# A state-space scan with a GELU feed-forward: another order of the steps, and the chunk-decay product in the y bank

## The chip, the cores and the metric

The kernel runs on one core of one Trainium2 chip. The metric is device time in microseconds (us), from one launch to its end. The engines are named as in the profile: PE (TensorE, with PEld for its weight loads), DVE (VectorE), ACT (ScalarE), POOL (GpSimd), and SP, which here only issues DMAs.

## The reference

A Mamba-2 style scan in chunks, for 4 batches and 8 heads over 768 positions (head size 32, state size 16), and then a feed-forward layer with the tanh form of GELU on the 3072 tokens of 256 features (hidden size 2048). Cut to what matters:

```python
cum = np.cumsum(log(clip(a)), axis=-1)                 # within a chunk
M = einsum('bhin,bhjn->bhij', C, B) * exp(cum_i - cum_j) * causal
y = M @ x + (C @ state) * exp(cum_i)
state = exp(sum(la)) * state + sum_j B_j x_j * exp(cum_end - cum_j)
h = y_as_tokens @ w_in
out = (0.5 * h * (1 + tanh(sqrt(2/pi) * (h + 0.044715 * h**3)))) @ w_out
```

## The kernel before

The scan uses chunks of 128 positions: 6 chunks for each batch, 24 in all, numbered `gc`. Two chunks are a unit `u` (0 to 11), three units a batch. The decays are folded into B and C by scaling them with running products of `a`, so each chunk needs only plain products. For a unit:

- `G.u` (L595): products of B and C, eight of 256 columns, into the banks `ga` and `gb`
- `M.u.0`, `M.u.1` (L605): DVE masks `ga` and `gb` with the triangle, into `m`
- `D.u` (L628): the chunk's contribution to the state; `S.u.k` (L674, L676) adds it to the decayed state and `SP.gc` (L683) makes the masked copy that the next chunk uses
- `Y.u` (L650, L659): y of both chunks, into the bank `yb`; `yev.u` copies it to `xm` (L666)
- `s1.u.i`, i from 0 to 7 (L709): first layer, four products of 256 columns into a buffer of the ring `hp` (two PSUM buffers); `gelu.u.i` (L713) takes it to `gT`
- `s2.u.k.q` (L727): second layer for chunk k, four products into the single buffer `o_ps` (or into `yb` for some late chunks); `oev.gc` copies it out and `store.gc` writes it

Units 0 and 1 have their own start. `XX.u` (L563) and `XD.u` (L573) unpack x and form the first state contributions for chunks 0 to 3, with copies `xn.c`; they take buffers of `hp` and `o_ps`. `tw` and `ew` transpose the scaled B and C of chunks 0 to 3; `GE` and `ME` (L610, L616) bring half of unit 0's mask through ACT and POOL. Chunks 4 and 5 come by `tp2`, `recip1`, `mul1.0`, `mul1.1`, `T1`, `bh1`, `ce1`, `N1` and `bn1`. `R` (L331) is the running product over `a`; `pe` (L385, L387), `pp` (L393) and `pend` form the decay of each whole chunk, spread over partitions by a product.

Batch 1 scales B and C with `mul.1.i` (L475) and turns them on PE (`T.1.i`, `E.1.i`, `N.1`, `bn.1`). Batches 2 and 3 turn them by way of memory: `store_s` (L497) writes the scaled tile to scratch, `turn_s` (L504) and `load_s` (L509) read it back turned and plain, `F` (L515) splits C by even and odd heads. The weights come in eight loads of 512 KB (`load_wi.q`, L190, `load_wo.q`, L194), each into a buffer of its own, and are cast to bf16 in halves (`wi.q.k`, `wo.q.k`). `castx.u` casts x.

The order of all this is written out by hand in the string `ORDERED`: the steps are issued in the sequence in which they stand there, and an engine runs its own in that sequence. `:A`, `:D` or `:P` behind a name puts the step on ACT, DVE or POOL. `~n` issues filler products of n times 128 columns into `yb` (L697); `+n` does so ahead of an `s1`, in its own buffer. A buffer's next user waits for the readers of the last.

Of the kernel before, what the change touches and what calls it, by code (L numbers as in the profile page):

```python
# [45 lines left out]
gelu.4.6 yev.5.0.2:D SP.12 s2.4.0.0.o s2.4.0.1.o s1.4.7 D.7 Y.6 G.7 gelu.4.7 load_bc.3.0 load_bc.3.1
mul.3.0 mul.3.1 S.7.0 S.7.1 load_x.9 s1.5.0 gelu.5.0 s2.4.0.2.o s2.4.0.3.o oev.8:A M.7.1
castx.8.None:A M.7.0 s1.5.1 s1.5.2 gelu.5.1 store_s.3.1 yev.6.0.2:D SP.14 s2.4.1.0.o s2.4.1.1.o
s1.5.3 gelu.5.2 s2.4.1.2.o s1.5.4 s2.4.1.3.o gelu.5.3 gelu.5.4 oev.9:A s1.5.5 D.8 Y.7 gelu.5.5
store_s.3.0 load_x.10 load_x.11 store.5 G.8 S.8.0 s1.5.6 s1.5.7 castx.9.None:D gelu.5.6 M.8.1  # L50
gelu.5.7 store.6 s2.5.0.0.o s2.5.0.1.o turn_s.3.0 s1.6.0 s1.6.1 s2.5.0.2.o s2.5.0.3.o gelu.6.0
gelu.6.1 oev.10:D SP.16 s1.6.2 s1.6.3 gelu.6.3 gelu.6.2 s2.5.1.0.o s2.5.1.1.o s2.5.1.2.o s2.5.1.3.o
load_s.3 store.9 turn_s.3.1 s1.6.4 s1.6.5 M.8.0 yev.7.0.2:A oev.11:A SP.15 store.8 gelu.6.4
s2.6.0.0.o F.3 s2.6.0.1.o gelu.6.5 s1.6.6 s1.6.7 gelu.6.6 Y.8 D.9 G.9 S.9.0 SP.18 S.9.1 store.7
gelu.6.7 s2.6.0.2.o s2.6.0.3.o castx.11.None:D oev.12:D s1.7.0 s1.7.1 s2.6.1.0.o gelu.7.0 s2.6.1.1.o
gelu.7.1 s1.7.2 s1.7.3 s2.6.1.2.o s2.6.1.3.o SP.19 oev.13:D M.9.0 gelu.7.2 M.9.1 castx.10.None:P
gelu.7.3 s1.7.4 s1.7.5 s2.7.0.0.o s2.7.0.1.o gelu.7.4 s1.7.6 gelu.7.5 yev.8.0.2:A s2.7.0.2.o s1.7.7
gelu.7.6 Y.9 D.10 S.10.0 S.10.1 G.10 gelu.7.7 M.10.0 s2.7.0.3.o yev.9.0.2:A oev.14:A s1.8.0 s1.8.1
s2.7.1.0.o s2.7.1.1.o gelu.8.0 gelu.8.1 SP.20 s1.8.2 s1.8.3 M.10.1 gelu.8.2 s2.7.1.2.o s2.7.1.3.o
gelu.8.3 s1.8.4 s1.8.5 Y.10 oev.15:A gelu.8.4 D.11 S.11.0 G.11 gelu.8.5 s1.8.6 store.15 s1.8.7  # L60
gelu.8.6 s2.8.0.0.o s2.8.0.1.o gelu.8.7 store.11 store.10 s1.9.0 gelu.9.0 s1.9.1 s2.8.0.2.o
s2.8.0.3.o gelu.9.1 M.11.1 M.11.0 oev.16:D SP.21 SP.22 yev.10.0.2:A s1.9.2 s1.9.3 gelu.9.2
s2.8.1.0.o s2.8.1.1.o gelu.9.3 s1.9.4 store.14 s1.9.5 gelu.9.4 s2.8.1.2.o s2.8.1.3.o gelu.9.5 s1.9.6
# [899 lines left out]
```

## Time and profile before

| | us |
|---|---|
| median of 3 runs | 117.64 |
| runs | 116.85 to 118.97 |
| span of the profiled execution | 115.1 |
| PE busy in it | 109.4 |
| ACT, DVE, POOL busy | 75.1, 68.7, 15.1 |

The span runs from the first to the last instruction of one profiled execution; the time of that execution as the runs count theirs is not recorded, and the median of the timed runs stands 2.5 us above the span. A row of a timeline gives start, length (from the first to the end of the last of a group), engine, line, operation, tiles and shapes, the count, and in brackets how long the engine was idle and what ended it. Starts and lengths are in us.

### The profile page before, as it was taken

To read this page: it belongs to the slowest core of one execution; us is meant where nothing else is said; L and a number is where in the kernel's file an instruction comes from. 1 tells how busy PE (TensorE), PEld (TensorE's weight loads), DVE (VectorE), ACT (ScalarE), POOL (GpSimd) and SP (SyncE) were. 2 spreads that over 40 slices of the span, in tenths; PEclk is the share of its full clock that TensorE was granted. 3 is DMA by queue.
4 is the path that set the end of the run, shared out by engine and by line. 5 is a ranking of instruction groups with operands and counts; after the bars stand their busy time and mean duration, and the time that the engine had idled before them with its cause. 6 is when DMAs were issued, how large, how long until landed. Compare 5 with 4: busy or idle time off the path is not lost.

```text
span 115.1 us, 3372 instructions
## 1 busy us (share of the span) xinstructions
PE 109.4 (95%) x1425; PEld 92.2 (80%) x1425; DVE 68.7 (60%) x135; ACT 75.1 (65%) x149; POOL 15.1 (13%) x32
## 2 busy tenths in 40 slices
PE   6999799999999999999999999999999999999990
...
DMA packets 43006, 15.97 MB, mean 139 GB/s; under 512 B 36656, under 2 KB 41456, under 8 KB 42992
## 3 DMA queue, kind: packets, MB, share of 16 engines
...
q10 hardware_dynamic: 144, 0.08, 0.4%
...
## 4 chain that ended last, share of the span: by engine, by line
PE 82%; DMA 8%; SPq 4%; POOL 1%; issue 1%; ACT 0%
PE hp L709 36%; PE o_ps L727 33%; DMA wf<-in_moe_w_out_dram 8%; PE yb L727 3%; PE ga L595 3%; PE yb L650 2%; PE yb L659 2%; SPq L190 1%; PE hp L628 1%; SPq L162 1%; SPq L159 1%; SPq L150 1%; POOL w_out_sb L316 1%; POOL w_in_sb L316 1%; SPq L183 1%
## 5 line engine op out<-in xcount | busy, mean ns | idle before, releaser
L713 ACT ACTIVATE gT<-hp 128x512 bf16<-128x512 f32 x96 | 53.3, 595 | 24.5 <-PE hp L709 24.0
L709 PE MATMUL hp<-xm,w_in_sb 128*128 128x256 bf16 x384 | 51.9, 273 | 0.5 <-ACT pend L314 0.3
L727 PE MATMUL o_ps<-w_out_sb,gT 128*128 128x256 bf16 x352 | 46.4, 273 | 0.0
L709 PEld LDWEIGHTS <-w_in_sb 128*128 128x128 bf16 x384 | 41.2, 114 | 3.2 <-issue 1.7
L727 PEld LDWEIGHTS <-gT 128*128 128x128 bf16 x384 | 37.0, 98 | 4.7 <-issue 0.8
L318 DVE COPY o_sb<-o_ps 128x256 f32<-128x256 f32 x7 | 3.0, 424 | 22.4 <-PE o_ps L727 18.4
L605 DVE TENSOR_TENSOR m<-ga,tri 128x1024 bf16<-128x1024 f32 x12 | 14.6, 1216 | 0.0
L605 DVE TENSOR_TENSOR m<-gb,tri 128x1024 bf16<-128x1024 f32 x11 | 13.4, 1219 | 0.5 <-PE gb L595 0.5
L697 PE MATMUL yb<-wz 128*128 128x512 bf16 (+2 forms) x24 | 8.2, 491 | 1.1 <-DVE warm L222 1.1
L314 ACT ACTIVATE o_sb<-o_ps 128x256 f32<-128x256 f32 x15 | 5.6, 382 | 4.1 <-PE o_ps L727 3.0
L683 DVE SCALAR_TENSOR_TENSOR sp_new<-s_new,pend,bmask 128x256 bf16<-128x256 f32 x17 | 8.0, 479 | 0.1
L316 POOL CAST x<-x_t 128x512 bf16<-128x512 f32 x5 | 3.2, 648 | 34.9 <-DMA x_t<-in_x_dram 22.9
L676 DVE SCALAR_TENSOR_TENSOR s_new<-s_new,pend,hp 128x64 f32<-128x64 f32 x13 | 3.6, 279 | 5.7 <-PE hp L628 5.5
L697 PEld LDWEIGHTS <-wz 128*128 128x128 bf16 x25 | 2.9, 126 | 5.0 <-issue 3.6
L659 PE MATMUL yb<-m,x 128*32 128x128 bf16 x192 | 6.1, 219 | 0.0
L650 PE MATMUL yb<-ce,sp_new 128*32 128x128 bf16 x160 | 5.3, 220 | 0.0
L595 PE MATMUL ga<-ce,bh 32*128 32x256 bf16 x48 | 4.7, 272 | 0.1
L314 ACT ACTIVATE xm<-yb 128x512 bf16<-128x512 f32 x8 | 4.8, 597 | 0.0
L595 PE MATMUL gb<-ce,bh 32*128 32x256 bf16 x48 | 4.7, 273 | 0.0
L727 PE MATMUL yb<-w_out_sb,gT 128*128 128x256 bf16 x32 | 4.1, 273 | 0.0
L659 PEld LDWEIGHTS <-x 128*32 128x32 bf16 x192 | 3.8, 97 | 0.4 <-issue 0.2
L650 PEld LDWEIGHTS <-sp_new 128*32 128x32 bf16 x160 | 3.0, 96 | 1.0 <-issue 1.0
...
## 6 DMA issues: line engine op xcount, KB each, us to landing
...
```

Of the source, the lines that this page charges most:

```text
L314: nc.scalar.activation(o, i, AF.Copy)
L316: nc.gpsimd.tensor_copy(out=o, in_=i)
L595: nc.tensor.matmul(out=gbank(g)[:, 256 * k:256 * k + 256], lhsT=bh_of(2 * u + k)[gs], rhs=ce_of(2 * u + k)[gs], start=True, stop=True, til ...
L605: nc.vector.tensor_tensor(out=m_of(u)[:, 2 * i:2 * i + 2].rearrange("p g k e t -> p (g k e) t"), in0=gx[i].rearrange("p g (k t) -> p (g k) ...
L650: nc.tensor.matmul(out=y4[32 * j:32 * j + 32, k, w], lhsT=sp[:, 32 * h:32 * h + 32], rhs=ce_of(gc)[:, h % 2], start=first(j), stop=False, ...
L659: nc.tensor.matmul(out=y4[32 * j:32 * j + 32, k, w], lhsT=X16[u][:, k, 32 * h:32 * h + 32], rhs=m[:, h // 2, h % 2, :], start=first(j), st ...
L676: nc.vector.scalar_tensor_tensor(out=s_new, in0=state[("s", gc - 1)], scalar=pend_of(gc), in1=d, op0=ALU.mult, op1=ALU.add)
L683: nc.vector.scalar_tensor_tensor(out=sp_new.rearrange("p (g d) -> p g d", g=4), in0=(XN[0][:, H * D:H * D + 64] if gc == 0 else state[("s" ...
L697: nc.tensor.matmul(out=t[:, 0:m * 128], lhsT=wz, rhs=w3.to_broadcast([128, m, 128]), start=True, stop=True, skip_group_check=True)
L709: nc.tensor.matmul(out=hp[:, j * T:(j + 1) * T], lhsT=w_in_k[:, w, q, k], rhs=xm[:, w, u * T:(u + 1) * T], start=(w == 0), stop=(w == 1))
L713: nc.scalar.activation(gts[u][:, 2 * i:2 * i + 2], hps.pop((u, i)).rearrange("p (j t) -> p j t", j=2), AF.Gelu_apprx_tanh)
L727: nc.tensor.matmul(out=ops[gc], lhsT=gts[u][:, fi, k * Q:(k + 1) * Q], rhs=w_out_sb[:, fi, :], start=(fi == 0 and (u > 0 or k == 0)), stop ...
```

## The change

The set of steps is the same. Three things differ:

- The order in `ORDERED` from `XD.0` on. The sequence on SP (all loads, stores and turns issued there) is unchanged, as is everything up to `XD.0`. On the other engines the steps stand in another sequence: `Y.0` ahead of `XX.1`; `R` ahead of `SP.0`; `pp` behind `s1.0.0`; `Y.1` ahead of `s1.0.4`; `mul.2.i` behind `SP.8` and `M.4.0`; `mul.3.i` still behind both halves of `M.6`, with `D.6`, `Y.5` and `G.6` later among the `s1` and `s2`; and so on. The filler of 13 goes from ahead of `G.1` to the end.
- `pp` writes its 24 columns to the bank `yb` instead of a buffer of the ring `hp`.
- Some copies and casts change engine: `wi.0.0`, `wi.1.0`, `wi.3.0`, `wo.1.1`, `wo.2.0`, `castx.6` from ACT to POOL; `wo.3.0`, `yev.1`, `yev.3`, `yev.10`, both `ce1`, and the copies out of chunks 3, 5, 6, 9, 11 and 18 from ACT to DVE; `wo.2.1`, `wo.3.1`, `castx.7` from POOL to ACT; `wi.3.1`, `castx.3`, `castx.10` from POOL to DVE; `bn.1`, `yev.4`, `yev.5`, `castx.11` and the copies out of chunks 10, 12 and 16 from DVE to ACT.

```diff
@@ -21,54 +21,55 @@
 c_sel c_warm c_m4 load_bc0.0 load_x4 clipq Rq tpq load_a.0:A load_a.1:S peq ~53 ppq pendq:A
 load_wi.0 c_cz c_bmask recip0 mulc.0:D mulc.1:D mulb:P ~9 tw.1 tw.0 ew.0.0:D c_par ew.0.1:A tw.2
 ew.0.2:A x4.1:D ~8 G.0 clip ew.1.0:A ew.1.1:A load_wi.1 M.0.0 GE.3 x4.0:P GE.2 load_wi.2 ~2 XX.0
-XD.0 load_wo.0 xn.0:A ew.1.2:A SP.0 S.0.0 xn.1:A wi.0.0:A wi.0.1:A R ~13 G.1 S.0.1 load_wi.3 XX.1
-load_bc1.0 xn.2:A ME.3:P ME.2:P pe Y.0 XD.1 pp yev.0.0.2:A S.1.0 load_wo.1 load_bc1.1 SP.1 S.1.1
-load_wo.2 wi.1.1:P M.1.0 wi.2.0:P wo.0.0:D pend:A wo.0.1:P wi.2.1:P SP.2 wi.1.0:A M.1.1 s1.0.0
-gelu.0.0 s1.0.1 gelu.0.1 xn.3:A wi.3.1:P s1.0.2+4 gelu.0.2 s1.0.3 s2.0.0.0.o load_wo.3 wo.1.0:P
-gelu.0.3 load_bc.1.0 s1.0.4 wi.3.0:A s1.0.5 gelu.0.4 Y.1 tp2 mul1.0 gelu.0.5 yev.1.0.2:A s1.0.6
-s1.0.7 gelu.0.6 load_x.2 tp6.0 load_bc.1.1 load_x.3 gelu.0.7 recip1 T1.0 s2.0.1.0.o s1.1.0 bh1:D N1
-s1.1.1 wo.1.1:A tp6.3 s2.0.0.1.o wo.2.1:P gelu.1.0 gelu.1.1 mul1.1 tp6.2 T1.1 tp6.1 ce1.1:A ce1.0:A
-wo.2.0:A bn1:D recip.1.4 s2.0.1.1.o s1.1.2 s1.1.3 gelu.1.2 wo.3.0:A wo.3.1:P G.2 gelu.1.3 s2.0.0.2.o
-s2.0.1.2.o s2.0.0.3.o castx.2.None:P s2.0.1.3.o load_bc.2.1 M.2.0 mul.1.0 M.2.1 oev.1:A s1.1.4
-s1.1.5 T.1.0 load_x.4 oev.0:A s2.1.0.0.o castx.3.None:P s2.1.0.1.o gelu.1.4 SP.3 D.2 gelu.1.5 s1.1.6
-S.2.0 SP.4 load_x.5 E.1.0:A N.1 mul.1.1 bn.1:D gelu.1.6 s1.1.7 Y.2 s2.1.0.2.o T.1.1 gelu.1.7
-yev.2.0.2:A s1.2.0 s1.2.1 gelu.2.0 E.1.1:D F.1 s2.1.0.3.o s1.2.2 gelu.2.1 gelu.2.2 D.3 load_bc.2.0
-oev.2:D G.3 S.3.0 S.3.1 s2.1.1.0.o load_x.6 castx.4.None:P s1.2.3 gelu.2.3 s2.1.1.1.o s2.1.1.2.o
-s1.2.4 M.3.1 M.3.0 gelu.2.4 SP.6 s2.1.1.3.o s1.2.5 oev.3:A gelu.2.5 D.4 Y.3 mul.2.1 S.4.0 G.4 s1.2.6
-s2.2.0.0.o SP.7 castx.5.None:A yev.3.0.2:A gelu.2.6 S.4.1 s1.2.7 mul.2.0 s2.2.0.1.o s1.3.0
-s2.2.0.2.o gelu.2.7 M.4.0 M.4.1 load_x.8 store_s.2.1 gelu.3.0 s1.3.1 s2.2.0.3.o s1.3.2 G.5 gelu.3.1
-SP.8 gelu.3.2 store_s.2.0 D.5 Y.4 M.5.1 oev.4:A S.5.0 s1.3.3 s2.2.1.0.o s2.2.1.1.o gelu.3.3 s1.3.4
...
+XD.0 load_wo.0 xn.0:A ew.1.2:A R SP.0 ME.3:P ME.2:P load_wi.3 xn.1:A G.1 S.0.0 S.0.1 M.1.0 Y.0
+wi.0.1:A XX.1 XD.1 yev.0.0.2:A S.1.0 pe M.1.1 SP.2 xn.2:A wi.0.0:P s1.0.0 pp s1.0.1 gelu.0.0 pend:A
+wi.1.0:P gelu.0.1 xn.3:A load_bc1.0 SP.1 load_wo.1 load_bc1.1 S.1.1 SP.3 wi.1.1:P s1.0.2+4 wi.2.1:P
+s1.0.3 wo.0.0:D gelu.0.2 wi.2.0:P Y.1 tp6.1 s1.0.4 gelu.0.3 load_wo.2 wo.0.1:P s1.0.5 wi.3.1:D
+gelu.0.4 wi.3.0:P gelu.0.5 s2.0.0.0.o s1.0.6 gelu.0.6 s1.0.7 gelu.0.7 s2.0.1.0.o yev.1.0.2:D s1.1.0
+gelu.1.0 tp2 mul1.0 recip1 T1.0 mul1.1 s1.1.1 T1.1 gelu.1.1 wo.1.0:P bh1:D N1 bn1:D s1.1.2 gelu.1.2
+ce1.1:D ce1.0:D wo.1.1:P s2.0.0.1.o s1.1.3 gelu.1.3 wo.2.1:A s1.1.4 gelu.1.4 G.2 load_wo.3
+load_bc.1.0 wo.3.1:A load_x.2 load_bc.1.1 load_x.3 s1.1.5 wo.2.0:P s2.0.1.1.o s2.0.0.2.o tp6.0 tp6.3
+M.2.0 wo.3.0:D gelu.1.5 s2.0.1.2.o s2.0.0.3.o s2.0.1.3.o oev.1:A s1.1.6 s1.1.7 tp6.2 oev.0:A
+gelu.1.6 castx.2.None:P s2.1.0.0.o mul.1.0 gelu.1.7 D.2 M.2.1 T.1.0 E.1.0:A s2.1.0.1.o S.2.0 SP.4
+Y.2 recip.1.4 yev.2.0.2:A s2.1.0.2.o s2.1.0.3.o mul.1.1 s1.2.0 s1.2.1 T.1.1 gelu.2.0 castx.3.None:D
+N.1 oev.2:D gelu.2.1 bn.1:A s1.2.2 s1.2.3 E.1.1:D gelu.2.2 F.1 gelu.2.3 s2.1.1.0.o s2.1.1.1.o D.3
+G.3 S.3.0 S.3.1 s1.2.4 gelu.2.4 s1.2.5 gelu.2.5 M.3.0 M.3.1 s2.1.1.2.o s2.1.1.3.o s1.2.6 gelu.2.6
+load_bc.2.1 load_x.4 load_x.5 s1.2.7 G.4 castx.5.None:A SP.6 gelu.2.7 oev.3:D Y.3 yev.3.0.2:D
+castx.4.None:P D.4 S.4.0 S.4.1 s2.2.0.0.o s2.2.0.1.o load_bc.2.0 SP.8 s1.3.0 s1.3.1 s2.2.0.2.o
+gelu.3.0 s2.2.0.3.o gelu.3.1 oev.4:A s1.3.2 s1.3.3 s2.2.1.0.o gelu.3.2 s2.2.1.1.o gelu.3.3 load_x.6
+load_x.8 mul.2.1 store_s.2.1 s1.3.4 gelu.3.4 M.4.0 s1.3.5 gelu.3.5 s2.2.1.2.o mul.2.0 s1.3.6
+store_s.2.0 SP.7 gelu.3.6 M.4.1 s2.2.1.3.o oev.5:D turn_s.2.1 D.5 Y.4 yev.4.0.2:A S.5.0 G.5 M.5.1
+s1.3.7 F.2 s1.4.0 s2.3.0.0.o s2.3.0.1.o gelu.3.7 gelu.4.0 store.1 s1.4.1 gelu.4.1 s1.4.2 s2.3.0.2.o
...
+s2.11.0.3.yb s2.11.1.0.o s2.11.1.1.o s2.11.1.2.o oev.22:A store.22 s2.11.1.3.o ~13 store.19 oev.23:A
+store.23
...
@@ -389,7 +390,7 @@
     def f_pp():
-        RP[2] = psh.tile([128, 512], FP32, name="hp")
+        RP[2] = yb
         nc.tensor.matmul(out=RP[2][:, 0:NCH], lhsT=selp[0:64].rearrange("p h n -> p (h n)"),
                          rhs=pe2.rearrange("p j c -> p (j c)"), start=True, stop=True,
                          skip_group_check=True)
@@ -793,7 +794,7 @@
     pd = add("A", f_pend, alt="AD", deps=[pp])
-    pp.takes("hp", pd)
+    pp.takes("yb", pd)
```

59 lines of the change are left out of this document (28 added, 31 removed).

## The prediction

> **What bounds the kernel now.** I read the page first (busy shares, slices), then the chain that ended last and the busy time by stretches (PE, PEld, DVE, ACT, POOL, then granted clock, DMA share, GB/s), then each engine's timeline over the first 30 us, since only there do the slices show holes.
>
> ```profile
> span 115.1 us, 3372 instructions
> PE 109.4 (95%) x1425; PEld 92.2 (80%) x1425; DVE 68.7 (60%) x135; ACT 75.1 (65%) x149; POOL 15.1 (13%) x32
> PE   6999799999999999999999999999999999999990
> ...
> 10.00:15.00 5.00, 4.18 (x124) 2.96 (x119) 3.83 (x11) 4.38 (x12) 2.32 (x4) 1.00 1.05 367
> 15.00:20.00 5.00, 4.50 (x66) 3.60 (x65) 4.89 (x10) 4.71 (x10) 2.91 (x5) 1.00 0.99 298
> 90.00:100.00 10.00, 10.00 (x119) 9.21 (x118) 1.97 (x5) 6.81 (x13) 0.00 (x0) 1.00 0.16 54
> ...
> 45.89 1.75 PE o_ps L727 x16
> 112.11 0.38 ACT o_sb L314
> ```
>
> The reader is to see a TensorE stream with no hole from 20 us to the last product; what follows it (a copy of 0.38 us at 112.11 and the last store) is the same in both kernels. Sixteen products of stage 2 take 1.75 us, so a step s1 or s2 (four products) is a slot of 0.437 us. The set of products is unchanged, so a reordering can gain only by filling holes between 10 and 20 us: there PE lacks 0.82 and 0.50 us, and some of its busy time is filler. It can lose wherever the new order opens a hole. The two kernels issue on SP in exactly the same sequence, and the loads of the first 30 us wait for no compute (eight weight buffers for eight loads), so I keep their landing times.
>
> **The front, part by part.** These are the rows of before that price it, PE first, then ACT, DVE, POOL.
>
> ```profile
> 10.40 0.88 PE L697 MATMUL yb<-wz 128*128 128x512 bf16 x4
> 11.36 0.28 PE L595 MATMUL ga<-ce,bh 32*128 32x256 bf16 x2
> 12.51 0.29 PE L659 MATMUL yb<-m,x 128*32 128x128 bf16 x8
> 13.49 0.40 PE L393 MATMUL hp<-pe,selp 64*128 64x24 f32 x2
> 14.18 1.03 PE L709 MATMUL hp<-xm,w_in_sb 128*128 128x256 bf16 x8 [0.28 <-ACT pend L314]
> 15.46 0.38 PE L697 MATMUL hp<-wz 128*128 128x512 bf16 x1 [0.25 <-ACT gT L713]
> 17.51 0.96 PE L709 MATMUL hp<-xm,w_in_sb 128*128 128x256 bf16 x7 [0.25 <-POOL w_in_sb L316]
> 18.95 1.06 PE L709 MATMUL hp<-xm,w_in_sb 128*128 128x256 bf16 x8
> 19.85 0.28 PE L443 MATMUL ga<-ident,bc0s 128*128 128x128 bf16 x2
> ...
> 10.93 0.38 ACT L314 ACTIVATE ce<-hp 128x256 bf16<-128x256 bf16 x1
> 11.78 1.15 ACT L314 ACTIVATE w_in_sb<-wf 128x512 bf16<-128x512 f32 x2 [0.19 <-DMA wf<-in_moe_w_in_dram]
> 13.10 0.59 ACT L314 ACTIVATE xm<-yb 128x512 bf16<-128x512 f32 x1
> 14.81 1.09 ACT L713 ACTIVATE gT<-hp 128x512 bf16<-128x512 f32 x2 [0.17 <-PE hp L709]
> ...
> 9.51 1.23 DVE L605 TENSOR_TENSOR m<-ga,tri 128x1024 bf16<-128x1024 f32 x1
> 11.07 0.48 DVE L683 SCALAR_TENSOR_TENSOR sp_new<-o_ps,pendq,bmask 128x256 bf16<-128x256 f32 x1 [0.33 <-ACT x L314]
> 11.60 0.94 DVE L331 TENSOR_TENSOR_SCAN r_t<-ac,ends 64x384 f32<-64x384 f32 x1
> 13.80 0.28 DVE L676 SCALAR_TENSOR_TENSOR s_new<-s_new,pendq,hp 128x64 f32<-128x64 f32 x1 [0.81 <-PE o_ps L573]
> 15.80 0.43 DVE L318 CAST w_out_sb<-wf 128x512 bf16<-128x512 f32 x1
> 16.14 0.83 DVE L683 SCALAR_TENSOR_TENSOR sp_new<-s_new,pendq,bmask 128x256 bf16<-128x256 f32 x1
> 18.14 0.99 DVE L342 STREAM_TRANSPOSE rt<-r_t 32x64 f32<-32x64 f32 x4
> 19.16 0.52 DVE L435 TENSOR_TENSOR bc0s<-bcf,rt 128x256 bf16<-128x256 f32 x1
> 20.17 0.42 DVE L318 COPY bh<-ga 128x256 bf16<-128x256 bf16 x1
> 42.63 0.68 DVE L318 CAST xm<-yb 128x512 bf16<-128x512 f32 x1
> ...
> 13.16 0.61 POOL L316 CAST w_in_sb<-wf 128x512 bf16<-128x512 f32 x1 [1.72 <-DMA wf<-in_moe_w_in_dram]
> 15.83 0.87 POOL L316 CAST w_out_sb<-wf 128x512 bf16<-128x512 f32 x1 [0.71 <-DMA wf<-in_moe_w_out_dram]
> 22.61 0.61 POOL L316 CAST w_out_sb<-wf 128x512 bf16<-128x512 f32 x1 [3.21 <-DMA wf<-in_moe_w_out_dram]
> 23.90 0.61 POOL L316 CAST w_out_sb<-wf 128x512 bf16<-128x512 f32 x1 [0.67 <-DMA wf<-in_moe_w_out_dram]
> ```
>
> *The filler of 13 ahead of G.1* (0.88 us) goes to the very end. That gains nothing: G.1 needs the second half of ew.1.2, which ends at 10.93 + 0.38 = 11.31, and G.1 starts at 11.36 with or without filler. At the end the four products run beside the last copy and store, which need longer than 0.88 us: cost 0.
>
> *Y.0 ahead of XX.1, R ahead of SP.0.* M.0.0 starts at 9.51; DVE's pitch behind it is some 0.1 under its 1.23, so R starts at 10.65 and SP.0 at 11.5, ending 11.99 (before: 11.55). The first eight products of Y.0 start at 11.65, the next need SP.0 (12.07), the last end at 12.5. Before they ended at 12.51 + 0.29 = 12.8: 0.3 us gained although SP.0 is later.
>
> *yev.0 ahead of xn.2, wi.0.0 to POOL.* ACT then has one weight cast (0.6 us from 11.78) in front of yev.0: it runs 12.5 to 13.1, before 13.10 to 13.69. XX.1 and XD.1 fit under it, as XD.1 no longer stands behind xn.2.
>
> *pp to the y bank, behind s1.0.0.* The hp ring has two buffers. Without pp, s1.0.0 takes the buffer that xn.1 and S.0.1 leave by 12.5, not the one that S.1.0 (13.80 + 0.28) left. So s1.0.0 starts at 13.15, before at 14.18: **1.03 us earlier**. The price: on DVE M.1.0 (pitch 1.14) now stands ahead of S.1.0 and pe; S.0.1 at 12.05, M.1.0 12.25, S.1.0 13.4, pe's two small products done at 13.95. pp is queued on PE behind s1.0.0, whose slot ends 13.59, and waits until 14.0: 0.4 lost, and its 0.33 (13.49 to the weight load at 13.82 in before) now lies inside the dense stream. s1.0.1 starts at 14.33, before 14.62. pp in the y bank must follow yev.0 (13.1) and be copied out before Y.1, 14.6 against 16: free.
>
> *gelu's hand-offs.* s1.0.0 ends at 13.75, gelu.0.0 at 14.4, so the filler of 4 needs no wait (before 15.46). s1.0.2 starts at 14.98, its casts wi.1.0 and wi.1.1 on POOL being done at 14.4 (0.61 each from a landing at 13.16). s1.0.3 waits for gelu.0.1 (14.93 + 0.03 + 0.59): 15.6.
>
> *Y.1 is late next.* It needs SP.1, which DVE reaches behind M.1.1 (13.95) and SP.2 (15.1). SP takes 0.48 us in the row at 11.07 but 0.83 at 16.14, where a POOL cast ran beside it and took 0.87 instead of 0.61. POOL now casts without a pause from 13.2 to 15.7, so I count one collision: 0.83 - 0.48 = 0.35 us. SP.1 is done at 16.3, Y.1 starts at 16.4 (16.05 without the collision, 16.75 with two). s1.0.4 and s1.0.5 follow without the wait for wi.2.1 (row 17.51, before), because the wi casts precede wo.0.1 on POOL; then s2.0.0.0, and s1.0.6 at 18.16 instead of 18.95: **0.79 us ahead**. Its casts wi.3.0 (POOL) and wi.3.1 (DVE) end at 17.7 and 18.05.
>
> *T1.0 is late after that.* Behind SP.1 DVE does S.1.1, SP.3, wo.0.0, one tp6, wi.3.1 and yev.1 (pitches 0.19 + 0.40 + 0.34 + 0.45 + 0.34 + 0.60 = 2.3 us: the rows' durations, or their like's, less the 0.08 by which neighbours overlap), so tp2 (1.02 to the next start) starts at 18.56 and mul1.0 (0.52) ends at 20.1, where before they began at 18.14 and ended at 19.68. PE has done s1.0.6, s1.0.7, s2.0.1.0 and s1.1.0 by 19.91 and waits until 20.2. Before, T1.0 ran at 19.85 with two slots fewer done: 19.85 + 0.87 - 20.2 = **0.52 us ahead**. N1 behind bh1 may cost another 0.2; before has as much in small gaps on the way to its next batch, so I set these against each other.
>
> *The late weights.* wo.2 and wo.3 land at 22.6 and 23.9 in either kernel. wo.2.1 and wo.3.1 now stand on ACT between gelu.1.3 and gelu.1.5, so gelu.1.4 is put off to 23.9 and gelu.1.5 to 25; their buffers are wanted by s1.1.6 and s1.1.7 at 25.5 and 26: hidden. wo.3.1 ends at 24.5, just as PE comes to s2.0.0.3 (24.6); the same held before (23.90 + 0.61). M.2.0, mul.1.0, D.2 and Y.2 come no later against their users.
>
> **The dense part.** I counted slots between each producer and consumer on PE in both orders. Copies of o_ps have 2 slots of cover at the least in both. From a Y to the s1 that its yev feeds there are 0.78 us at the tightest before (Y.2) and 0.77 after (Y.4, Y.5); a copy of 0.59 (ACT, row 13.10) fits, and in before no hole shows there. I cost it at 0.
>
> The scratch round trip is what the fixed SP order drags along (DVE and chain rows):
>
> ```profile
> 54.74 0.96 DVE L475 TENSOR_TENSOR bc<-bc_t,pt 128x768 bf16<-128x768 f32 x1 [0.30 <-DMA bc_t<-in_C_dram]
> 68.37 0.75 DVE L515 TENSOR_SCALAR ce<-ch,par 128x768 bf16<-128x768 bf16 x2 [0.43 <-DMA ch<-scr]
> 71.41 0.21 PE ga L595 x2
> ```
>
> mul.3.1 now stands behind both M.6 and ends at about 57.7 (before 55.7); store_s, turn_s and load_s behind it, and every DMA after them in SP's queue, move by these 2.0 us, and F.3 would run at 70.4 instead of 68.4. G.9, its user, stands 2.8 us later in PE's order (slots counted), so 73.6 instead of 71.3: the cover of 2.2 us stays. Batch 2 is alike: mul.2.x some 2.5 us later, G.6 5.0 us later in slots. Casts that change engine among ACT, DVE and POOL after 30 us have spare engines (row 90 to 100: DVE 1.97 of 10 us): 0.
>
> **The sum.** Of 1.03 us at s1.0.0, 0.5 us is left in the dense stream. The profiled execution spans 115.1 us, so 114.6; the median of the runs shown is 117.64, 2.5 us above the span, and I carry the difference over: **117.1 us**. Bounds: no collision on DVE adds 0.35 of gain (116.8); the last three waits gone as well gives the whole 1.03 (116.6); two collisions leave 0.15 (117.5).
>
> **Rivals.**
> *More than that.* If pp, Y.1, T1.0 all meet less wait than worked out, the most is PE's missing 1.32 us with both fillers (0.88 + 0.21): 2.4 us, 115.2. Against it: DVE was busy 4.89 of 5 us from 15 to 20 already, and it gets more. Its likely form is 116.4.
> *Hidden anyway.* The early lead is handed back at T1.0, N1 and wo.3's landing, and the end stays: 117.6. For it: the DVE list to mul1.0 is longer than before by 0.4 us.
> *DVE becomes the bound (slower).* From 13 to 24 us DVE takes over wi.3.1, yev.1, both ce1 and wo.3.0 (0.34 + 0.60 + 2 x 0.42 + 0.34 = 2.1 us), while POOL casts beside it. G.2 then hangs on ce1.0 at 22.45, with PE there at 22.9. Each further collision adds 0.35 us; three of them use up the 0.45 of cover and the 0.5 of gain, and at five (1.75) the time is 117.1 + 1.3 = 118.4, slower than before. For it: the rows 0.83 and 0.87. Against it: only one such pair shows in before, in a stretch where POOL was busy 2.91 of 5 us. [...]
> *The clock falls (slower).* Between 10.5 and 14.3 the new order leaves PE idle for about half the time, no filler covering it. The first products of before show what a slow array costs:
>
> ```profile
> 1.05 5.76 PE L697 MATMUL yb<-wz 128*128 128x512 bf16 x14 [1.05 <-DVE warm L222]
> 6.85 0.65 PE L697 MATMUL yb<-wz 128*128 128x512 bf16 x3
> ```
>
> 14 products took 5.76 us, 0.41 each, later ones 0.22 each, though the granted clock reads 1.00 throughout: half speed for nearly 6 us. Were that paid again from 13 us, half of 5.76 is lost: 117.1 + 2.9 = 120.0. Against it: the longest single gap is 0.88 us. [...] No row here shows a fall in mid-kernel.
>
> **Chances.** Forecast (116.6 to 117.4) 0.50; more than that 0.15; hidden anyway 0.17; DVE bound 0.13; clock 0.05. 2% of 117.64 is 2.35 us, about what a measurement of this kernel can tell from no change. Faster by more (under 115.3) needs nearly every hole closed: 0.06, inside the first rival. Slower by more (over 120.0) takes the clock or a DVE bound with a missed batch 3 on top: 0.09. Within 2%: 0.85. The range for eight in ten reaches to the likely form of the first rival, with the spread of the runs shown, and to the DVE bound: 116.0 to 118.4; the likeliest case alone is 116.6 to 117.4, signs being mixed.
>
> **What would show it.** The first product of s1 at about 13.2 with yev.0 as releaser; pp behind it with a wait of about 0.4 on DVE's pe; Y.1 at 16.1 to 16.7 waiting for DVE; T1.0 at about 20 waiting for mul1.0; from 21 us on no PE gap; the last copy at about 111.6. Wrong would be: a late first s1, a gap at G.2, G.6, G.9 or s2.0.0.3, s1 products at twice their length, or weight landings that moved.

## The result, and the profile after

In six runs each, side by side, the changed kernel ("after") takes 118.63 us (117.7 to 119.19) and the kernel before 117.82 us (116.85 to 118.97): a ratio of 1.0115, 95% interval 1.007 to 1.016. It is about 1% slower. The forecast was 117.1 us, 0.5 us faster, and its range ended at 118.4. The profiled execution of after took 118.76 us with a span of 117.0: what lies around the span is 1.8 us, not the 2.5 us that the forecast carried over. A ratio here leaves out executions more than 1.5% above the fastest of their kernel (of b_nofill below, five of twelve).

From the page of after: its span, the busy sums, and the granted clock in 40 slices.

```profile
span 117.0 us, 3366 instructions
PE 112.0 (96%) x1425; PEld 93.0 (79%) x1425; DVE 72.4 (62%) x143; ACT 73.1 (62%) x141; POOL 15.5 (13%) x32
PEclk9999657999999999999999999999999999999999
```

The same 1425 products are busy for 2.6 us longer than in before (109.4), and the clock row, all nines before, falls in slices 5 to 7, from about 12 to 20 us. The busy time by stretches of after says more (columns as in the prediction: PE, PEld, DVE, ACT, POOL, then the granted clock, DMA share, GB/s). The rows from 9.00 to 19.25 are cut where the clock changes.

```profile
10.00:15.00 5.00, 3.90 (x115) 2.03 (x109) 4.47 (x10) 3.08 (x9) 4.04 (x6) 0.74 1.07 367
...
9.00:12.42 3.42, 2.28 (x82) 1.36 (x81) 3.32 (x7) 3.09 (x9) 2.19 (x3) 1.00 1.02 329
12.42:15.83 3.41, 3.41 (x64) 1.93 (x52) 2.99 (x7) 1.72 (x4) 2.58 (x5) 0.50 1.08 356
15.83:19.25 3.42, 3.42 (x41) 2.18 (x42) 2.81 (x7) 2.06 (x4) 1.76 (x3) 0.50 0.93 278
...
26.00:60.00 34.00, 34.00 (x464) 29.78 (x462) 28.14 (x46) 23.90 (x46) 1.26 (x3) 1.00 0.70 148
60.00:110.00 50.00, 50.00 (x656) 45.03 (x655) 22.52 (x39) 34.16 (x65) 0.00 (x0) 1.00 0.28 69
```

From 12.42 to 19.25 us the array runs at half clock; from 26 to 110 us PE has no hole, as before. So nearly all that was lost was lost in the front. The timeline of after shows where (PE rows, then DVE, POOL and ACT).

```profile
11.37 0.28 PE L596 MATMUL ga<-ce,bh 32*128 32x256 bf16 x2 [0.89 <-ACT ce L315]
12.15 0.24 PE L660 MATMUL yb<-m,x 128*32 128x128 bf16 x4 [0.22 <-POOL m L617]
13.91 1.04 PE L710 MATMUL hp<-xm,w_in_sb 128*128 128x256 bf16 x4
16.70 1.91 PE L710 MATMUL hp<-xm,w_in_sb 128*128 128x256 bf16 x8
20.76 1.06 PE L710 MATMUL hp<-xm,w_in_sb 128*128 128x256 bf16 x8
22.53 0.28 PE L444 MATMUL ga<-ident,bc0s 128*128 128x128 bf16 x2
...
9.52 1.23 DVE L606 TENSOR_TENSOR m<-ga,tri 128x1024 bf16<-128x1024 f32 x1
14.46 0.17 DVE L388 TENSOR_TENSOR pe<-pe,m 64x24 f32<-64x24 f32 x1
21.43 0.42 DVE L436 TENSOR_TENSOR bc0s<-bcf,rt 128x256 bf16<-128x256 f32 x1
...
10.23 1.87 POOL L617 TENSOR_SCALAR_AFFINE_SELECT m<-ge 128x512 bf16<-128x512 bf16 x2 [1.71 <-ACT ge L611]
...
114.06 0.38 ACT L315 ACTIVATE o_sb<-o_ps 128x256 f32<-128x256 f32 x1 [1.36 <-PE o_ps L728]
```

Where the filler stood, PE now idles 0.89 us ahead of G.1. Eight products of s1 take 1.91 us at half clock (row 16.70) and 1.06 at full clock (row 20.76). s1.0.6 starts at 20.76; before at 18.95, so the forecast lead of 0.79 us is a lag of 1.81. T1.0 (22.53) has two slots more behind it than in before (19.85 + 0.87 = 20.72): the lag is still 1.81, and at the last copy, 114.06 against 112.11, it is 1.95.

In this execution it is the slow products that hold PE: from 13.91 us to T1.0 no product waits for another engine, and mul1.0, on which T1.0 depends, ends at 21.43 + 0.42 = 21.85, 0.68 us ahead of T1.0. Whether the order would have lost without them is asked in a_fill below.

Three distances measure each kernel: from the mask product M.0.0 (first row of DVE above) to T1.0, the front; from T1.0 to the last copy, the rest; and the time. With 0.87 us added to the front of before for its two slots, and taken from its rest, before has 11.21 and 91.39 us and after 13.01 and 91.53. Executions differ by up to 0.8 us in when M.0.0 starts (9.37 to 10.17), so the front is counted from there.

### The profile page after: what moved, and what is told of

The parts are those of the page before. It is cut to its first block, busy times and chain, and to the rows that moved or that the text cites. A ratio compares the mean times of both kernels' runs of the same rounds, so it can differ in the third digit from the quotient of the medians.

```text
span 117.0 us, 3366 instructions
## 1 busy us (share of the span) xinstructions
PE 112.0 (96%) x1425; PEld 93.0 (79%) x1425; DVE 72.4 (62%) x143; ACT 73.1 (62%) x141; POOL 15.5 (13%) x32
## 4 chain that ended last, share of the span: by engine, by line
PE 88%; POOL 2%; ACT 1%; DVE 1%; issue 0%
PE hp L710 38%; PE o_ps L728 33%; PE yb L728 3%; PE yb L660 3%; PE ga L596 3%; PE yb L651 2%; POOL m L617 2%; PE hp L629 1%; PE hp L564 1%; DVE cz L410 1%; PE yb L698 1%; ACT ce L315 1%; PE hp L426 1%; ACT ge L611 0%; PE yb L394 0%; PE ga L485 0%
## 5 line engine op out<-in xcount | busy, mean ns | idle before, releaser
L710 PE MATMUL hp<-xm,w_in_sb 128*128 128x256 bf16 x384 | 53.8, 279 | 0.0
L728 PE MATMUL o_ps<-w_out_sb,gT 128*128 128x256 bf16 x352 | 47.3, 273 | 0.0
L710 PEld LDWEIGHTS <-w_in_sb 128*128 128x128 bf16 x384 | 41.7, 115 | 3.0 <-issue 0.8
L319 DVE COPY o_sb<-o_ps 128x256 f32<-128x256 f32 x10 | 4.2, 422 | 18.3 <-PE o_ps L728 18.3
L315 ACT ACTIVATE o_sb<-o_ps 128x256 f32<-128x256 f32 x12 | 4.5, 382 | 4.7 <-PE o_ps L728 3.7
L660 PE MATMUL yb<-m,x 128*32 128x128 bf16 x192 | 6.6, 226 | 0.2 <-POOL m L617 0.2
L315 ACT ACTIVATE xm<-yb 128x512 bf16<-128x512 f32 x7 | 4.2, 598 | 2.0 <-PE yb L660 1.5
L319 DVE CAST xm<-yb 128x512 bf16<-128x512 f32 x5 | 3.4, 684 | 1.3 <-PE yb L660 1.0
```

What stands on the lines that cost most here:

```text
L315: nc.scalar.activation(o, i, AF.Copy)
L319: nc.vector.tensor_copy(out=o, in_=i)
L660: nc.tensor.matmul(out=y4[32 * j:32 * j + 32, k, w], lhsT=X16[u][:, k, 32 * h:32 * h + 32], rhs=m[:, h // 2, h % 2, :], start=first(j), st ...
L710: nc.tensor.matmul(out=hp[:, j * T:(j + 1) * T], lhsT=w_in_k[:, w, q, k], rhs=xm[:, w, u * T:(u + 1) * T], start=(w == 0), stop=(w == 1))
L728: nc.tensor.matmul(out=ops[gc], lhsT=gts[u][:, fi, k * Q:(k + 1) * Q], rhs=w_out_sb[:, fi, :], start=(fi == 0 and (u > 0 or k == 0)), stop ...
```

## The experiments

The theory after the result was the clock, and its rival the hand-offs of the new order. From x_act on the theory is that DVE's list, stretched by POOL's casts, is the bound. All kernels but after ran in five rounds beside before, whose median was 117.1 to 117.5 in them.

| kernel | us, median (lowest to highest) | ratio to before [95%] | front | rest |
|---|---|---|---|---|
| before | 117.2 in the first batch (116.48 to 119.79, and one of 220.12) | | 11.21 | 91.39 |
| after | 118.63 (117.7 to 119.19) | 1.0115 [1.007, 1.016] | 13.01 | 91.53 |
| a_fill | 118.66 (118.32 to 118.67) | 1.0138 [1.0104, 1.0172] | 12.71 | 91.69 |
| a_noend | 118.58 (118.0 to 118.88) | 1.013 [1.0086, 1.0174] | 12.32 | 91.66 |
| b_nofill | 118.07 (116.77 to 119.24) | 1.0028 [0.9988, 1.0067] | 12.85 | 91.38 |
| a_fill_R | 118.33 (117.88 to 118.95) | 1.0118 [1.0078, 1.0159] | 12.85 | 91.53 |
| x_act | 118.13 (117.59 to 119.01) | 1.0079 [1.0051, 1.0107] | 11.84 | 91.52 |
| x_pe | 118.13 (117.61 to 119.24) | 1.0085 [1.005, 1.0119] | 12.05 | 91.69 |
| x_list | 117.13 (116.76 to 117.76) | 0.9998 [0.9974, 1.0021] | 11.01 | 91.87 |
| x_best | 117.8 (117.26 to 118.68) | 1.0036 [1.0003, 1.0069] | 11.63 | 91.88 |
| b_eng | 119.6 (118.83 to 120.72) | 1.0194 [1.0153, 1.0235] | 12.12 | 92.91 |
| v1 | 117.07 (116.7 to 118.31) | 0.9999 [0.9968, 1.003] | 11.26 | 91.52 |
| v2 | 117.62 (117.18 to 118.44) | 1.005 [1.002, 1.008] | 10.96 | 92.41 |
| v3 | 117.01 (116.75 to 117.75) | 0.9968 [0.9934, 1.0002] | 11.15 | 91.52 |

Front and rest are of one profiled execution each; in those of b_nofill and b_eng 0.87 us is moved from the rest to the front as for before.

### The filler back: a_fill

```diff
-... xn.1:A G.1 S.0.0 S.0.1 M.1.0 Y.0
+... xn.1:A ~13 G.1 S.0.0 S.0.1 M.1.0 Y.0
...
-... store.22 s2.11.1.3.o ~13 store.19 oev.23:A
+... store.22 s2.11.1.3.o store.19 oev.23:A
```

> The changed kernel with its filler of 13 put back ahead of G.1 and taken off the end. [...] Rival (order): the hand-offs of the new order cost the time and the clock is beside the point; then this stays at 118.3 to 118.8, 0.5 us or more above before, with the clock at 1.00.

The clock stays up (0.996 to 1.0 in all six runs). The clock theory had the time back at before's or under it; it does not come back: 118.66 us, as the rival had it. So the fall of the clock is not needed for the loss. What holds this kernel can be read now that the products run at full speed. PE, DVE and POOL of a_fill's timeline:

```profile
13.37 0.63 PE L710 MATMUL hp<-xm,w_in_sb 128*128 128x256 bf16 x4
14.83 0.40 PE L394 MATMUL yb<-pe,selp 64*128 64x24 f32 x2 [0.83 <-DVE pe L388]
15.16 0.63 PE L710 MATMUL hp<-xm,w_in_sb 128*128 128x256 bf16 x4
17.40 0.30 PE L651 MATMUL yb<-ce,sp_new 128*32 128x128 bf16 x8 [0.33 <-DVE sp_new L684]
19.30 0.27 PE L710 MATMUL hp<-xm,w_in_sb 128*128 128x256 bf16 x1
20.20 0.96 PE L710 MATMUL hp<-xm,w_in_sb 128*128 128x256 bf16 x7 [0.62 <-DVE w_in_sb L319]
22.27 0.28 PE L444 MATMUL ga<-ident,bc0s 128*128 128x128 bf16 x2 [0.24 <-DVE bc0s L436]
...
10.70 1.01 DVE L332 TENSOR_TENSOR_SCAN r_t<-ac,ends 64x384 f32<-64x384 f32 x1
13.84 0.35 DVE L386 TENSOR_TENSOR pe<-ac,r_t 64x3 f32<-64x3 f32 x1
14.22 0.55 DVE L388 TENSOR_TENSOR pe<-pe,m 64x24 f32<-64x24 f32 x1
14.70 1.21 DVE L606 TENSOR_TENSOR m<-gb,tri 128x1024 bf16<-128x1024 f32 x1
15.83 1.51 DVE L684 SCALAR_TENSOR_TENSOR sp_new<-s_new,pendq,bmask 128x256 bf16<-128x256 f32 x2
17.57 0.83 DVE L684 SCALAR_TENSOR_TENSOR sp_new<-s_new,pend,bmask 128x256 bf16<-128x256 f32 x1
19.32 0.82 DVE L319 CAST w_in_sb<-wf 128x512 bf16<-128x512 f32 x1
...
13.57 1.17 POOL L317 CAST w_in_sb<-wf 128x512 bf16<-128x512 f32 x2 [0.87 <-DMA wf<-in_moe_w_in_dram]
14.93 1.39 POOL L317 CAST w_in_sb<-wf 128x512 bf16<-128x512 f32 x2 [0.19 <-DMA wf<-in_moe_w_in_dram]
16.27 0.80 POOL L317 CAST w_out_sb<-wf 128x512 bf16<-128x512 f32 x1
17.52 0.61 POOL L317 CAST w_in_sb<-wf 128x512 bf16<-128x512 f32 x1 [0.45 <-DMA wf<-in_moe_w_in_dram]
19.25 1.36 POOL L317 CAST w_out_sb<-wf 128x512 bf16<-128x512 f32 x2 [1.12 <-DMA wf<-in_moe_w_out_dram]
```

Each of PE's four waits behind s1.0.0 names DVE, 0.83 + 0.33 + 0.62 + 0.24 = 2.02 us. And DVE is late because its steps are longer beside POOL's casts (R beside its selects, ME): pe 0.35 + 0.55 us instead of 0.15 + 0.18 in before, the pair of SP 1.51 instead of 0.88, SP.3 0.83 instead of 0.48, the cast wi.3.1 0.82 instead of 0.42, R 1.01 instead of 0.94: 2.0 us in sum. POOL's two casts beside the second pe product end at 13.57 + 1.17 = 14.74, and the product itself at 14.22 + 0.55 = 14.77. The mask product at 14.70, which reads one operand from PSUM, takes 1.21 us beside the casts of 14.93; M.0.0 took 1.23 in before, with POOL idle for its first 0.7 us.

### The filler away, the rest as before: b_nofill

```diff
-... wi.0.1:A R ~13 G.1 S.0.1 load_wi.3 XX.1
+... wi.0.1:A R G.1 S.0.1 load_wi.3 XX.1
...
-... s2.11.1.3.o oev.23:A store.23
+... s2.11.1.3.o ~13 oev.23:A store.23
```

> The kernel before with only its filler of 13 moved from ahead of G.1 to the end; everything else as before. Theory (clock): the same hole opens at 10.4 us, the granted clock falls to a half for one or two windows in many executions, and the time rises by 0.7 to 2 us, to 118.5 to 119.8. Rival (order): the filler only covers a wait, so the time stays that of before, 117.8 within 0.3 us.

The profiled execution has the half clock too, from 12.42 to 19.24 us:

```profile
14.41 1.87 PE L709 MATMUL hp<-xm,w_in_sb 128*128 128x256 bf16 x8 [0.28 <-ACT pend L314]
```

Its executions fall into kinds: with a mean clock of 0.971, as in the profiled one with its 6.82 us at half speed, six of the twelve take 118.46 to 119.24 us; with 0.985, which comes to half as long, five take 117.0 to 117.69; and the one at 1.0 takes 116.77. The median of all twelve is 0.9 us above before's. So with the filler away the clock often falls, and in before's order, where no wait on DVE hides the slow products, 6.8 us at half clock cost some 1.7 us against the execution with none. Either cause is thus enough for a loss of this size, DVE's list in a_fill and the clock here, and in after the two lie over each other: with the clock held, a_fill has a front only 0.3 us shorter than after.

The filler makes the fall rarer and does not rule it out. The mean clock was under 0.99 in three of six executions of after, in four of six of a_noend and in eleven of twelve here, all without filler ahead of G.1; with it, in 12 of the 90 executions of before in these batches, in four of six of a_fill_R and in two of six of b_eng, and in none of the other kernels.

### No filler at all: a_noend

```diff
-... store.22 s2.11.1.3.o ~13 store.19 oev.23:A
+... store.22 s2.11.1.3.o store.19 oev.23:A
```

> The changed kernel without the filler of 13 at its end (four products whose result nothing reads are left out). Both theories: the time of the changed kernel, 118.6 within 0.4 us, since the products run beside the last copy and store. If the end filler costs something, it is 0.3 us or more under that. It also gives another execution of the changed order: by the clock theory it again shows half clock between 12 and 20 us in some executions, and those without it are the faster ones by 1 us or more; by the rival they are alike.

118.58 us against 118.63: the filler at the end is free, as costed. Its runs at full clock take 118.0 and 118.09 us, those with a mean clock of 0.985 or 0.971 118.44 to 118.88: half clock costs this order some 0.7 us. That is less than the 1 us or more of the clock theory, and more than the nothing of its rival.

### R back behind SP.0 and S.0.0: a_fill_R

```diff
-... ew.1.2:A R SP.0 ME.3:P ME.2:P load_wi.3 xn.1:A ~13 G.1 S.0.0 S.0.1 M.1.0 Y.0
+... ew.1.2:A SP.0 ME.3:P ME.2:P load_wi.3 xn.1:A ~13 G.1 S.0.0 R S.0.1 M.1.0 Y.0
```

> The changed kernel with the filler of 13 back ahead of G.1, and R again behind SP.0 and S.0.0 on DVE as before. The scan R ran beside the two selects ME on POOL, which took 1.87 us instead of 1.22, so that Y.0 waited for them until 12.15. If R is what slows them, ME takes about 1.25 us here, Y.0 ends 0.3 to 0.4 us earlier and the time is 0.2 to 0.4 us under that of the same kernel with R first; if POOL's length has another cause, it stays at 1.87 and the times agree within 0.2 us.

ME takes 1.23 us again instead of 1.87, Y.0 waits for nothing, and s1.0.0 starts at 13.15, as the prediction had it. The time, 118.33 us, is 0.33 below a_fill's, within the 0.2 to 0.4 expected. But R now stands where POOL casts (11.41 to 12.02), and pp waits 1.36 us for pe instead of 0.83: part of what the order gains at one place of DVE's list it loses at the next. The T1.0 of this execution, at 22.38, is not to be compared with a_fill's: the clock was down from about 15.5 to 19.0 us (0.66 on the mean of 15 to 20), and T1.0 waited for no engine.

### Casts off POOL: x_act

```diff
-... xn.2:A wi.0.0:P s1.0.0 pp s1.0.1 gelu.0.0 pend:A
-wi.1.0:P gelu.0.1 ... SP.3 wi.1.1:P s1.0.2+4 wi.2.1:P
+... xn.2:A wi.0.0:P wi.1.0:A s1.0.0 pp s1.0.1 gelu.0.0 wi.1.1:A pend:A
+gelu.0.1 ... SP.3 s1.0.2+4 wi.2.1:A
...
-s1.0.3 wo.0.0:D gelu.0.2 wi.2.0:P Y.1
+s1.0.3 wo.0.0:D gelu.0.2 wi.2.0:A Y.1
```

> The changed kernel with its filler ahead of G.1 (clock held at 1.00), and the four casts wi.1.0, wi.1.1, wi.2.1, wi.2.0 on ACT instead of POOL; DVE's list is untouched. Theory (collision): POOL casts stretch the DVE operations with two SBUF operands that run beside them; without them pe takes 0.15 + 0.17 us (0.90 with them), SP.2 and SP.1 together 0.9 (1.51), Y.1 starts by 16.5 (17.4), T1.0 by 21.4 (22.3), and the time is 117.4 to 118.0 instead of 118.66. Rival (list): DVE simply has too many steps ahead of mul1.0; then these lengths stay, or T1.0 stays at 22.0 to 22.4, and the time stays within 0.3 of 118.66.

With POOL idle from 13.2 to 15.7, pe is back at its own length, and SP.3, with a cast still beside it at first, as well (DVE rows of x_act):

```profile
14.35 0.15 DVE L386 TENSOR_TENSOR pe<-ac,r_t 64x3 f32<-64x3 f32 x1
14.53 0.17 DVE L388 TENSOR_TENSOR pe<-pe,m 64x24 f32<-64x24 f32 x1
15.76 1.22 DVE L684 SCALAR_TENSOR_TENSOR sp_new<-s_new,pendq,bmask 128x256 bf16<-128x256 f32 x2
17.56 0.48 DVE L684 SCALAR_TENSOR_TENSOR sp_new<-s_new,pend,bmask 128x256 bf16<-128x256 f32 x1
```

The front is 0.87 us shorter than a_fill's, the time 0.5 us; most of the difference is the M.0.0 of this execution, 0.5 us later. The time, 118.13 us, lies between what the theory expected (up to 118.0) and the rival (118.36 and more). Not all comes back: the pair of SP meets wo.0.1, wi.3.1 and yev.1 stand on DVE as before, and ACT becomes late with wi.2.0 (s1.0.4 waits 0.65 us for it).

### pe ahead of the mask product: x_pe

```diff
-... S.0.0 S.0.1 M.1.0 Y.0
+... S.0.0 S.0.1 pe M.1.0 Y.0
...
-... yev.0.0.2:A S.1.0 pe M.1.1 SP.2 xn.2:A wi.0.0:P s1.0.0
+... yev.0.0.2:A S.1.0 M.1.1 SP.2 xn.2:A wi.0.0:P s1.0.0
```

> The changed kernel with the filler ahead of G.1, and pe ahead of M.1.0 on DVE. pp no longer waits on PE (0.83 us there), s1.0.1 starts at about 13.9 instead of 15.2. If the wait of pp costs what PE loses by it, the time falls by 0.6 to 0.9, to about 117.9. If DVE's chain to SP.1 and mul1.0 is the bound (theory), pe is only moved within the same list: Y.1 stays at 17.2 to 17.5, T1.0 at 21.9 to 22.3, and the time stays at 118.3 to 118.7.

pp waits for nothing, yet s1.0.1 starts no earlier: it waits 0.39 us for xn.2 on ACT, and that waited for DVE (ACT row of x_pe):

```profile
14.80 0.38 ACT L315 ACTIVATE x<-hp 128x256 bf16<-128x256 f32 x1 [0.98 <-DVE s_new L677]
```

xn.2 and S.1.0 read one PSUM buffer, and xn.2, which stands later in the written order, waited 0.98 us for S.1.0 here: in the prediction xn.2 was free. The casts now fall beside other steps (the pair of SP 1.40, wo.0.0 0.83, mul1.0 0.73), and T1.0 waits 0.55 us for mul1.0. T1.0 comes at 22.13, as the theory had it; the time, 118.13 us, lies between the two expectations (117.9, and 118.3 or more).

### Two casts off DVE's list: x_list

```diff
-... s1.0.5 wi.3.1:D
-gelu.0.4 wi.3.0:P gelu.0.5 s2.0.0.0.o s1.0.6 ... s2.0.1.0.o yev.1.0.2:D s1.1.0
+... s1.0.5 wi.3.1:A
+gelu.0.4 wi.3.0:P gelu.0.5 yev.1.0.2:A s2.0.0.0.o s1.0.6 ... s2.0.1.0.o s1.1.0
```

> The changed kernel with the filler ahead of G.1, and two steps off DVE's list ahead of mul1.0: wi.3.1 and yev.1 go to ACT, where ACT is idle (yev.1 behind gelu.0.5). POOL is untouched, so the collisions up to SP.1 stay (1.5 us for the SP pair, Y.1 at 17.4). If DVE's list is the bound behind Y.1, the wait for wi.3.1 on PE (0.62) goes, T1.0 comes at 20.8 to 21.3 instead of 22.3 and the time falls by 0.8 to 1.2, to 117.5 to 117.9. If not, it stays within 0.3 of 118.66.

This brings back the whole loss, more than expected: 117.13 us, ratio 0.9998. It is a_fill but for the engine of two casts and the place of one of them, yev.1. mul1.0 runs right behind the transposes, 2.0 us sooner after M.0.0 than in a_fill (where it starts at 21.79), and T1.0 waits for nothing (x_list's DVE and PE rows):

```profile
18.86 1.51 DVE L343 STREAM_TRANSPOSE rt<-r_t 32x192 f32<-32x192 f32 x5
20.40 0.42 DVE L436 TENSOR_TENSOR bc0s<-bcf,rt 128x256 bf16<-128x256 f32 x1
...
21.18 0.28 PE L444 MATMUL ga<-ident,bc0s 128*128 128x128 bf16 x2
```

Of the 1.70 us by which its front is shorter than a_fill's, 1.10 lie between Y.1 and T1.0 (4.87 to 3.77 us), where the two casts stood. The other 0.60 lie ahead of Y.1, where nothing that the edit touches runs, so they are no gain of it: M.0.0 stands 0.61 us later in this execution, while POOL's casts from wi.1.0 on start within 0.12 us of a_fill's and so meet other steps of DVE's list (pe took 0.41 + 0.17 us here). The execution shown, 117.74 us, is the second slowest of the twelve.

### All of these together: x_best

x_pe and x_list together, wi.2.0 and wi.2.1 on ACT, and SP.1 ahead of SP.2:

```diff
-... load_bc1.0 SP.1 load_wo.1 load_bc1.1 S.1.1 SP.3 wi.1.1:P s1.0.2+4 wi.2.1:P
-s1.0.3 wo.0.0:D gelu.0.2 wi.2.0:P Y.1
+... load_bc1.0 SP.1 SP.2 load_wo.1 load_bc1.1 S.1.1 SP.3 wi.1.1:P s1.0.2+4 wi.2.1:A
+s1.0.3 wo.0.0:D gelu.0.2 wi.2.0:A Y.1
```

> All at once, on the changed kernel with the filler ahead of G.1: pe ahead of M.1.0, SP.1 ahead of SP.2, wi.2.0, wi.2.1, wi.3.1 and yev.1 on ACT; wi.1.0 and wi.1.1 stay on POOL, beside the mask products M, which read one operand from PSUM. By the theory (DVE bound, made longer by POOL casts) no DVE operation is stretched before 16 us, Y.1 starts by 16.4, T1.0 by 20.3, as was forecast for the change, and the time is 116.3 to 117.0, at or under the kernel before (117.2 to 117.8). If it stays above 117.6, something other than DVE's list and its collisions holds PE, such as ACT, which gets 2.4 us more.

DVE is as light as wished (the pair of SP in 0.87 us, mul1.0 at 18.95, 0.8 us sooner after M.0.0 than in x_list), and the time is 117.8 us, 0.7 us worse than x_list. It lies above the 117.6 from which the expectation names ACT, and ACT holds PE now (the first wait is for xn.2, as in x_pe):

```profile
14.70 0.60 PE L710 MATMUL hp<-xm,w_in_sb 128*128 128x256 bf16 x4 [0.39 <-ACT x L315]
17.78 1.08 PE L710 MATMUL hp<-xm,w_in_sb 128*128 128x256 bf16 x8 [0.64 <-ACT w_in_sb L315]
```

### The engine moves alone: b_eng

Before's order, with the early casts and copies on the engines that the change gives them (`wi.0.0`, `wi.1.0`, `wi.3.0`, `wo.1.1`, `wo.2.0` on POOL, `wi.3.1`, `yev.1`, both `ce1`, `wo.3.0` on DVE, `wo.2.1`, `wo.3.1` on ACT):

```diff
-... xn.1:A wi.0.0:A wi.0.1:A R ~13 G.1 S.0.1 load_wi.3 XX.1
+... xn.1:A wi.0.1:A R ~13 G.1 S.0.1 load_wi.3 XX.1
-load_bc1.0 xn.2:A ME.3:P ME.2:P pe Y.0 ...
+load_bc1.0 xn.2:A ME.3:P ME.2:P wi.0.0:P pe Y.0 ...
...
```

> The kernel before in its own order, with only the engines of the early casts and copies as in the changed kernel (wi.0.0, wi.1.0, wi.3.0, wo.1.1, wo.2.0 on POOL; wi.3.1, yev.1, both ce1, wo.3.0 on DVE; wo.2.1, wo.3.1 on ACT; wi.0.0 stands behind ME and wi.1.0 behind wi.1.1, so that POOL's queue is not blocked). Theory (DVE's list ahead of mul1.0 and T1.0, stretched by POOL casts, is the bound): DVE gets 1 to 2 us more before T1.0 and G.2, and the time rises by 0.6 to 1.5 us, to 117.8 to 118.7. Rival (the order of the steps does it, whatever the engines): the time stays at 117.2 within 0.3.

119.6 us, the slowest of all and above what either side expected, and its profile is at full clock: the new order isn't needed for the loss. With these engines for the early casts the new order is no slower than the old one (a_fill's ratio is 1.0138, this one's 1.0194, with intervals that overlap). Of the loss against before 0.9 us lie in the front and 1.5 behind T1.0. Four of the seven rows on what PE waited for, in b_eng, from 10 to 30 us (who waits, for whom: us in total, times, longest):

```profile
PE hp L393 <- DVE pe L387: 1.3, 1, 1.3
PE ga L595 <- DVE bn L318: 0.6, 1, 0.6
PE hp L709 <- POOL w_in_sb L316: 0.5, 1, 0.5
PE ga L463 <- DVE bh L318: 0.2, 1, 0.2
```

Of these four waits before has only the third, at 0.3 us. The second is G.2's, behind T1.0. pe took 0.49 + 0.55 us.

### Can the order gain? v1, v2, v3

v1 is x_list with pe ahead of M.1.0, SP.1 ahead of SP.2, and xn.2 ahead of S.1.0 so that ACT doesn't wait:

```diff
-... S.0.0 S.0.1 M.1.0 Y.0
-wi.0.1:A XX.1 XD.1 yev.0.0.2:A S.1.0 pe M.1.1 SP.2 xn.2:A wi.0.0:P s1.0.0 ...
+... S.0.0 S.0.1 pe M.1.0 Y.0
+wi.0.1:A XX.1 XD.1 yev.0.0.2:A xn.2:A S.1.0 M.1.1 wi.0.0:P s1.0.0 ...
...
-wi.1.0:P gelu.0.1 xn.3:A load_bc1.0 SP.1 load_wo.1 ...
+wi.1.0:P gelu.0.1 xn.3:A load_bc1.0 SP.1 SP.2 load_wo.1 ...
```

> On the changed kernel: filler ahead of G.1, wi.3.1 and yev.1 on ACT (as in the run that came out level with the kernel before), and in addition pe ahead of M.1.0, xn.2 ahead of S.1.0 (the two read the same PSUM tile, and the later in program order waits for the earlier), SP.1 ahead of SP.2. Theory: the waits of PE for pe (0.5), for xn.2 (0.4) and for SP.1 (0.2) go, T1.0 moves up by 0.4 to 0.8, and the time is 116.4 to 116.9, under the kernel before. If DVE's length alone decides, it stays at 117.0 to 117.3, since DVE does as much as before.

A miss: 117.07 us, no better than x_list. pp and s1.0.1 wait for nothing, Y.1's second half waits 0.19 us for SP.2, and the rest of the lead lasts until s1.0.6 waits for ACT, which cast wi.3.1 ahead of gelu.0.4 (PE row of v1):

```profile
19.06 1.08 PE L710 MATMUL hp<-xm,w_in_sb 128*128 128x256 bf16 x8 [0.30 <-ACT gT L714]
```

v2 is v1 with a transpose of the running products, tp6.1, put off:

```diff
-... wi.2.0:P Y.1 tp6.1 s1.0.4
+... wi.2.0:P Y.1 s1.0.4
...
-M.2.0 wo.3.0:D gelu.1.5
+M.2.0 tp6.1 wo.3.0:D gelu.1.5
```

> The same, with one of the four wide turns (tp6, 0.51 us on DVE) put off from ahead of tp2 to behind M.2.0. If DVE's list ahead of mul1.0 is what holds T1.0, this gives up to another 0.4 us: 116.1 to 116.7. If PE's own slots or ACT hold it by now, it equals the run without it within 0.2.

A miss too, and worse: the transpose, put off, stands ahead of the cast wo.3.0 on DVE, and s2.0.0.3 waits 0.73 us for that (PE row of v2):

```profile
26.79 0.38 PE L728 MATMUL o_ps<-w_out_sb,gT 128*128 128x256 bf16 x2 [0.73 <-DVE w_out_sb L319]
```

v3 is v1 with gelu.0.4 ahead of wi.3.1, s2.0.1.0 ahead of s1.0.6, and wo.3.0 ahead of M.2.0:

```diff
-... s1.0.5 wi.3.1:A
-gelu.0.4 wi.3.0:P gelu.0.5 yev.1.0.2:A s2.0.0.0.o s1.0.6 gelu.0.6 s1.0.7 gelu.0.7 s2.0.1.0.o s1.1.0
+... s1.0.5 gelu.0.4 wi.3.1:A
+wi.3.0:P gelu.0.5 yev.1.0.2:A s2.0.0.0.o s2.0.1.0.o s1.0.6 gelu.0.6 s1.0.7 gelu.0.7 s1.1.0
...
-M.2.0 wo.3.0:D gelu.1.5
+wo.3.0:D M.2.0 gelu.1.5
```

> v1 was level with before although DVE no longer held PE. Its trace shows one hole left that the order makes: s2.0.0.0 ends its slot at 18.6 and s1.0.6 starts at 19.06, since ACT ran wi.3.1 (17.89, behind an idle time of 0.87 us on the landing of wi.3) ahead of gelu.0.4, whose buffer s1.0.6 takes. v3 is v1 with gelu.0.4 ahead of wi.3.1, s2.0.1.0 ahead of s1.0.6, and the cast wo.3.0 ahead of M.2.0 on DVE so that the time saved is not given back at s2.0.0.3. Theory (the front is a list of engine work, and PE takes what the lists leave): the hole of 0.46 us closes, s1.0.6 starts at about 19.05 with s2.0.1.0 done, T1.0 at about 20.5 against a first mask product M.0.0 at 9.7, and the time is 116.6 to 116.8 (ratio 0.996). Rival (the end of the front is set by the landing of the late weights): s2.0.0.3 waits for a cast of wo.3 by as much as was saved, and the time stays at 117.1 (ratio 1.000). If v2's loss of 0.5 us came from tp6.1 standing ahead of wo.3.0 on DVE (its trace shows PE waiting 0.73 us for that cast), v3 shows no such wait.

The hole named is closed, and another stands 1.4 us later: s1.1.0 waits for gelu.0.6, which ACT runs behind wi.3.1 and yev.1 (PE row of v3):

```profile
20.09 0.60 PE L710 MATMUL hp<-xm,w_in_sb 128*128 128x256 bf16 x4 [0.38 <-ACT gT L714]
```

There is no wait for wo.3. The time, 117.01 us, ratio 0.9968 [0.9934, 1.0002], can't be told from before's, and is above the 116.6 to 116.8 expected. The ratio comes near the 0.996 expected in part because before was slower in this batch (117.54 us; the clock fell in six of its 17 executions, and in none of v3's).

No kernel here beats before by more than its interval.

## Why the prediction was wrong, step by step

Two steps failed, the count of collisions on DVE and the cost of the filler. The prediction assumed full clock, so its steps are read in a_fill, whose M.0.0 is 0.05 us later than before's.

| step | predicted | a_fill, less 0.05 | slip added |
|---|---|---|---|
| s1.0.0 | 13.15 | 13.32 | 0.17 |
| s1.0.1, behind pp | 14.33 | 15.11 | 0.61 |
| Y.1 | 16.4 | 17.35 | 0.17 |
| s1.0.6, its first product | 18.16 | 19.25 | 0.14 |
| hole ahead of its second | none | 20.20 - 19.30 - 0.11 | 0.79 |
| T1.0 | 20.2 | 22.22 | 0.14 |

*The step that failed* is "I count one collision (0.35 us)" in the part on Y.1, and with it the list to mul1.0, which was added up from undisturbed pitches. DVE's steps from R to wi.3.1 were stretched by 2.0 us where 0.35 was counted. At T1.0 the forecast lead of 0.52 us is a lag of 1.50 (front 12.71 against 11.21), and the 2.0 us between them are the 2.02 of the table. Collisions not counted make up 1.7 of them. The other 0.4 come from the pitches behind SP.1: the prediction took 0.08 us of overlap off each, but in a_fill SP.3, tp6.1, wi.3.1 and tp2 each start 0.03 or 0.04 us after the step ahead of them ends. The mechanism stood there, as the rival in which DVE becomes the bound, with 118.4 us and a chance of 0.13; a_fill, with the clock held, came out at 118.66. It had the place wrong: G.2, where it looked for the wait, waits for nothing, and the waits stand at pp, Y.1, s1.0.6 and T1.0. That after itself, with the clock fallen as well, comes so near its 118.4 is partly luck. The evidence held against it, that before shows one such pair, was weak: in before POOL idles 1.72 us ahead of 13.16 and again between its casts, and the change itself takes POOL's busy time from 10 to 15 us from 2.32 to 4.04 us.

What the stretched steps read can be told in a_fill: pe, SP.1 to SP.3 and R, whose operands all lie in SBUF, and the cast wi.3.1 from SBUF were stretched (pe's second product from 0.18 us in before to 0.55, ending 0.03 us from the casts' end), and the mask product with one operand in PSUM was not (1.21 us). The price of one was about right: 0.37 us for that pe product, 0.35 for SP.3 and 0.40 for wi.3.1, where 0.35 was put. It was the number of such steps that failed.

*The filler* "gains nothing" was right for its own time, and its end costs nothing (a_noend). But taking it from ahead of G.1 was costed at nothing, and that step failed: without it there the clock fell in 18 of 24 executions. The rival "the clock falls", with a chance of 0.05, had the place about right (10.5 to 14.3; the fall is at 12.42), and its sign, s1 products at twice their length, came true. What the prediction held against it, a longest gap of 0.88 us, was no safeguard: in after the longest gap ahead of the fall was 0.89. Its price, 2.9 us, was too high: half clock cost some 0.7 us in a_noend and some 1.7 in b_nofill. In after part of it lies over DVE's waits. With the filler gone and x_list's two casts moved, the clock should show; that kernel was not run.

*Y.0 and s1.0.0* came 0.17 us late, because the scan R, moved beside ME, stretches ME from 1.22 to 1.87 us and Y.0 waits 0.22 for it: a collision that was not looked for. a_fill_R has neither.

*xn.2* was taken as free, but waits for S.1.0 (0.98 us on ACT in x_pe, 0.39 of them on PE): a small term, hidden behind pe until pe is moved.

*The late weights, the dense part, the round trip by way of memory and the casts after 30 us* were costed at 0: the rest is 91.53 us against 91.39 (91.69 in a_fill). Right, within 0.14 to 0.30.

*"I carry the difference over"* (2.5 us above the span): with 1.7 to 1.8 us around the span, as in every later run but b_eng's (2.0), the sum would have been 116.4, farther off. By the same 1.7 to 1.8 the profiled execution of before, with a span of 115.1, took some 116.85 us, the lowest of the runs shown, and not their median.

What stays open: why runs of after at full clock spread from 117.7 to 118.77 us, and a_noend's stand at 118.0 and 118.09, while a_fill's lie at 118.32 to 118.67. The collisions differ between executions (pe took 0.15 + 0.17 us in the profile of after and 0.35 + 0.55 in that of a_fill). The author's guess is that they hang on when a weight lands against when DVE gets there, but no run held the landings fixed.
